# Inverse transform of a two-part kernel: a fourth table buffer, two units prepared ahead, constants and two operand stacks loaded at another time

## The chip, the cores and the metric

The kernel runs on one core of a Trainium2 chip. A core has five engines that work side by side, each in the order of its own instructions: TensorE (PE, matrix products into PSUM), VectorE (DVE), ScalarE (ACT), GpSimd (POOL) and SyncE (SP). Sixteen DMA engines move data between main memory and SBUF; in this kernel their transfers are issued by SP and by POOL. The metric is the device time in microseconds of one execution; lower is better. A profile of one execution shows what each engine did and when.

## The reference

Two independent computations share one output row. Part A is a linear-memory attention over four segments of 512 positions with 32 heads of 18 columns, part B a two-dimensional Fourier filter:

```python
# A: x @ wq, x @ wk, x @ wv, per head and segment s of four
logits = einsum("bhqd,bhkd->bhqk", qs, ks) * scale + mask
a_dot  = einsum("bhqk,bhkd->bhqd", softmax(logits), vs)
a_mem  = (phi(qs) @ M) / (phi(qs) @ z + 1e-6)      # M, z: sums over the segments before
o      = g * a_mem + (1 - g) * a_dot               # then @ wo
# B: x is 2048 x 576
X = rfft2(x) * (w_r + 1j * w_i)
y = irfft2(X, s=(2048, 576))
return concatenate([a, b], axis=-1)
```

## The kernel before

The whole program is one hand-ordered stream: generators yield between small steps, and the order in which they are drained is the order of each engine's instructions. There are four stages.

1. *Forward transform* (`FFT.forward`): 16 units, matrix products with cosine and sine tables; single-precision values are carried as a high and a low part, so that each product is three.
2. *Projections* (`ATT.projections`): for each of four segments g, nine units of queries and keys (`qk_unit`) and four blocks of values (`v_unit`), 13 units i in all. Between them the VectorE steps of the transform's middle part run as a paced background (`Pace`), the last of them the butterflies `FFT.last`, which finish the array Z in four batches b = 0..3 (`s.done` tells the last one that is finished). At unit i = 9 of segment 3 the function `hook` opens the pools of the inverse and calls `inv_setup`, which issues the transfers of two small tables and of the first per-unit tables `civ` on POOL's queue (lines 257 to 267).
3. *Inverse transform* (`FFT.inverse`, from line 284): 16 units u. Unit u takes the four-by-four entry of Z that belongs to it. `ysplit(u)` (line 275) writes its high part with two ACT copies (line 280) and its low part with two POOL subtractions (line 281); three sets of these tiles Y exist. `i2` (18 matmuls, line 296) multiplies them with the unit's table `civ` into PSUM, ACT and DVE take the result out as a high and a low part T, and two units later `i3` (14 matmuls, line 307) transforms back; ACT and DVE form the output rows, SP stores them. After unit u's second `i2` the table of unit u+3 is asked for (`load_civ`, a POOL issue); there are three table buffers. `ysplit(u+2)` is issued within unit u. The tile `p` of `i2` has two PSUM buffers under the tag `i2`, `i3`'s has two others under `i3`.
4. *Attention*: 16 stacks n of eight heads. A stack is `Qs` (110 rows) and `Ks` (110 rows), each filled by six SP transfers of 18 rows by eight heads (`stack_dmas`, issue at line 608) from the projections' result in main memory. Rows 0 to 107 hold three bfloat16 parts of the values; rows 108 and 109 hold the row maxima (`Qs`, written by `mpath`, POOL issue at line 657) and constants of -1 (`Ks`, line 558). There are three `Qs` and four `Ks` buffers. `s1(t)` computes the scores of head t for the maxima (PE line 624 and 633, with DVE at 628 and 634), `s2(t)` computes them again with the maxima subtracted and takes the exponential (lines 667 to 679).

The first ten calls of `s1` belong to stacks 0 and 1 and run during the inverse: `prologue` issues the twelve loads of stack 0 in one go before the first inverse unit; from unit 3 on, at three of the four yields of each unit, it is advanced by one step, and every `s1(t)` has three steps, 30 in all. Before the first `s1` step it calls `masks` (two ACT casts of a mask and an identity that PE's line 633 reads). At two of every three steps it takes one transfer from a list q: both halves of stack 1, the `Ks` half of stack 2, and the values of stack 1. `att_setup`, ahead of the inverse's first unit, issues the four constants of -1 on POOL's queue.

`attention` then runs 133 steps t. Eight steps belong to a stack; at each stack's first step the loads of `Qs` for stack n+2, of `Ks` for n+3 and of the values for n+2 are put into a list from which two are issued in each step. The scores `s1(t+10)` run ten steps ahead, so step 6 of the attention is the first that reads stack 2.

The lines that set this order are `if i>5 and i%4!=3: next(pr,None)` in `emit`, and `if q and i%3<2: q.pop(0)()` in `prologue`.

Of the kernel before, what the change touches and what calls it, by code (L numbers as in the profile page):

```python
# [5 lines left out]
F32=mybir.dt.float32; F32R=mybir.dt.float32r  # L6
# [96 lines left out]
class FFT:  # L103
# [152 lines left out]
    def inv_setup(s,cp):  # L256
        nc,io=s.nc,s.io
        s.cp=cp; s.civ={}
        s.itab=cp.tile([128,2,2,2,FP],F32R,name="itab",bufs=1); s.itab2=cp.tile([128,2,FP],F32R,name="itab2",bufs=1)
        nc.gpsimd.dma_start(s.itab,io["itab"].rearrange("p (h r c f) -> p h r c f",h=2,r=2,c=2))  # L260
        nc.gpsimd.dma_start(s.itab2,io["itab2"].rearrange("p (r f) -> p r f",r=2))
        for u in range(3): s.load_civ(u)
    def load_civ(s,u):
        b,a=divmod(u,4)
        cc=s.cp.tile([128,2,384],F32R,name="civ",bufs=3)
        s.nc.gpsimd.dma_start(cc,s.io["civ"][4*a+b].rearrange("p (h m) -> p h m",h=2))
        s.civ[u]=cc
    def last(s):
# [14 lines left out]
    def inverse(s,yl,pp):  # L283

        nc,io=s.nc,s.io; tab,tab2=s.itab,s.itab2; v=nc.vector
        T={}; po={}; Yt=s.Yt
        def i2(u,cs):
            Y=Yt[u]; cc=s.civ[u]
            p=pp.tile([128,len(cs),256],F32,name="i2",tag="i2")
            for k,c in enumerate(cs):  # L290
                n=0
                for (i,hl) in ((0,0),(0,1),(1,0)):
                    for q in range(2):
                        o=128 if q==0 else 0
                        m=128 if c<2 else 99
                        nc.tensor.matmul(p[:m,k],Y[i][:,q,c*128:c*128+m],cc[:,hl,o:o+256],start=n==0,stop=n==5)  # L296
                        n+=1
            return p
        def i3(u):
            h,l=T.pop(u); po[u]=[]  # L300
            for r in range(2):
                p=pp.tile([128,FP],F32,name=f"i3{r}",tag="i3"); po[u].append(p)
                w=slice(r*128,(r+1)*128)
                L=[(h[:,0,w],tab[:,0,r,0]),(h[:,1,w],tab[:,0,r,1]),(h[:,0,w],tab[:,1,r,0]),(h[:,1,w],tab[:,1,r,1]),
                   (l[:,0,w],tab[:,0,r,0]),(l[:,1,w],tab[:,0,r,1]),(h[:99,2,w],tab2[:99,r])]
                for n,(x,t) in enumerate(L):
                    nc.tensor.matmul(p,x,t,start=n==0,stop=n==6)  # L307
                yield
        def out(u):
            b,a=divmod(u,4); p=po.pop(u)  # L310
            E=yl.tile([128,FP],F32,name="E")
            nc.scalar.copy(E,p[0])
            o=yl.tile([128,2,FP],F32,name="yout",bufs=3)
            v.tensor_tensor(o[:,0],E,p[1],op=OP.add)
            v.tensor_tensor(o[:,1],E,p[1],op=OP.subtract)
            pend.append(lambda: nc.sync.dma_start(io["yb"][4*a+b],o))
        pend=[]
        def flush():
            while pend: pend.pop(0)()
        for u in range(18):  # L320
            if u>15: flush()
            if u<16:
                h=yl.tile([128,3,256],F32R,name="T0",bufs=3); l=yl.tile([128,2,256],F32R,name="T1",bufs=3)
                T[u]=(h,l)
                p=i2(u,(0,1))
                nc.scalar.copy(h[:,:2],p)
                if u+2<16: s.ysplit(u+2)
                v.tensor_tensor(l,p,h[:,:2].bitcast(F32),op=OP.subtract)
                yield
                flush()  # L330
                p=i2(u,(2,))
                Yt.pop(u); s.civ.pop(u)
                nc.scalar.copy(h[:99,2],p[:99,0])
                v.tensor_tensor(h[64:97,2],p[64:97,0],h[64:97,2].bitcast(F32),op=OP.subtract)
                if u+3<16: s.load_civ(u+3)
                yield
            if u>1:
                yield from i3(u-2)
                out(u-2)
                s.pace.take(1)  # L340
        flush()
# [35 lines left out]
class ATT:  # L377
# [176 lines left out]
    def att_setup(s,cp):  # L554
        nc,io=s.nc,s.io
        s.Qs=[cp.tile([128,8,512],BF,name=f"Qs{i}") for i in range(3)]
        s.Ks=[cp.tile([128,8,512],BF,name=f"Ks{i}") for i in range(4)]
        for i in range(4): nc.gpsimd.dma_start(s.Ks[i][108:110].rearrange("p h c -> p (h c)"),io["neg1"])
        s.mask=cp.tile([128,512],F32,name="mask"); nc.sync.dma_start(s.mask,io["mask"]); s.tri=cp.tile([128,128],BF,name="tri"); s.idb=cp.tile([128,128],BF,name="idb")
        s.bt,s.gt,s.g1=[cp.tile([128,1],F32,name=n) for n in ("bt","gt","g1")]  # L560
        nc.sync.dma_start(s.bt,io["beta"])
        d=lambda n,sh,dt: s.dp.tile(sh,dt,name=n)
        s.uD=[d(f"uD{i}",[576,512],F32) for i in range(4)]
        s.rD=[d(f"rD{i}",[32,512],F32) for i in range(4)]
        nc.sync.dma_start(s.rD[3][24:32],io["neg1"][0:1].rearrange("o (h c) -> (o h) c",c=512))
        s.dD=[None]+[d(f"dD{i}",[32,512],F32) for i in range(1,4)]
        s.rrD=[d(f"rrD{i}",[64,512],F32) for i in range(4)]
        s.rdD=[None]+[d(f"rdD{i}",[64,512],F32) for i in range(1,4)]
# [284 lines left out]
    def prologue(s):  # L853

        nc,io=s.nc,s.io
        for f in s.stack_dmas(0,0)+s.stack_dmas(0,1): f()
        yield
        s.load_v(0)
        q=s.stack_dmas(1,0)+s.stack_dmas(1,1)+s.stack_dmas(2,1)+[lambda: s.load_v(1)]
        for i in range(2): yield  # L860
        s.masks()
        i=0
        for t in range(10):
            for _ in s.s1(t):
                if q and i%3<2: q.pop(0)()
                i+=1
                yield
            if t in (3,7): m=s.mpath(t//4); next(m)
            if t in (4,8): next(m); next(m,None)
        assert not q  # L870
# [3 lines left out]
    def attention(s,tp,ps):  # L874
# [7 lines left out]
        q=[]  # L882
# [11 lines left out]
        for t in range(133):  # L894
            k,hh=divmod(t,4); n,qd=divmod(k,2); g=k//8
            if hh==0 and qd==0:
                if n+2<16: q+=s.stack_dmas(n+2,0)
                if n+3<16: q+=s.stack_dmas(n+3,1)
                if n+2<16: q.append(lambda n=n: s.load_v(n+2))
            st=t%32  # L900
            if 16<=t<21: s.pq_load(1,t-16)
            if t==34: bg.append(s.den(1,lane))
            if st==8 and g>0:
                def ln(g=g):
                    r=s.recip(s.rD[g-1],s.rrD[g-1],s.g1,False,"rr",2)
                    for i in range(8):
                        next(r); yield
                    for u in range(3): s.ux_load(g-1,u)
                    yield from r
                    bg.append(s.combine(g-1))  # L910
                    for u in range(5 if g<4 else 0): bg.append(s.mem1(g,u))
                    if g<3: bg.append(s.den(g+1,lane))
                    bg.append(s.oproj(g-1))
                lane.append(ln())
            if t==125: lane.append(s.recip(s.rD[3],s.rrD[3],s.g1,False,"rr"))
            a=s.s1(t+10) if t+10<128 else iter(())
            b=s.s2(t) if t<128 else iter(())
            if q: q.pop(0)()
            if qu: qu.pop(0)()
            steps(a,1)  # L920
            steps(b,1)
            steps(a,1)
            steps(b,1)
            if 4<=t-1<132: s.pv((t-5)//4,(t-5)%4)
            run_bg(1.2)
            steps(a,1)
            if hh==3 and m is not None: steps(m,1)
            steps(b,1)
            if hh==3 and m is not None: steps(m,1)
            if hh==1 and k+2<32: m=s.mpath(k+2); next(m)  # L930
            if t>=8 and t%4==0:
                s.pv_out((t-8)//4)
                if t%8==4:
                    u=s.u_dmas((t-12)//8)
                    if t<124: s.later(1,lambda u=u: qu.extend(u))
                    else: qu+=u
            for l in list(lane):
                try: next(l)
                except StopIteration: lane.remove(l)
            if q: q.pop(0)()  # L940
            if qu: qu.pop(0)()
            run_bg(0)
            s.due(t)
# [6 lines left out]
        i=0  # L950
# [59 lines left out]
def emit(nc,tc,io):  # L1010
    def pool(es,name,bufs=1,**kw):
        return es.enter_context(tc.tile_pool(name=name,bufs=bufs,reuse_waits="tile",**kw))
    with ExitStack() as L0:
# [9 lines left out]
        with tc.manual_schedule():  # L1023
# [5 lines left out]
            with ExitStack() as es:  # L1029
# [3 lines left out]
                def hook(g,i):  # L1033
                    if g==3 and i==9:
# [2 lines left out]
                        F.yp=pool(Ri,"yp",2); F.Yt={}; ci=pool(Ri,"ci")  # L1037
                        tc.swap_default_side()
                        F.inv_setup(ci)
                A.projections(xp,tp,pp,wv,F.pace,hook)  # L1040
                F.ysplit(0); F.ysplit(1)
            Rv.close(); L1x.close()
            with ExitStack() as L1:
                cp2=pool(L1,"cp2"); sm=pool(L1,"sm",2); sp=pool(L1,"sp",3)
# [33 lines left out]
```

## Time and profile before

| | us |
|---|---|
| three runs | 777.62, 773.33, 770.01 (median 773.33) |
| the profiled execution | 769.95 |
| its span, first to last instruction | 768.2 |
| forward transform (0 to 76.1) | 76.1 |
| projections (76.1 to 284.4) | 208.3 |
| inverse transform with the first scores (284.4 to 370.9) | 86.5 |
| attention with its last projection (370.9 to 768.2) | 397.3 |

The stage bounds are read from the timeline: the first matmul of each stage on PE, or the end of the last one of the stage before. The granted clock of TensorE was 0.989 over the span. Within the inverse PE was busy 76.53 of the 86.5 us, in the projections 206.26 of 208.3.

In the profile L296 means line 296 of the kernel; the names behind an operation are output <- inputs, by the program's names. PE is the matmuls, PEld the weight loads beside them, SPq and POOLq the issue of transfers on the queues of SP and POOL. In a timeline row the first two numbers are the start and the time taken (several instructions of one kind are merged, "x18"), and a bracket tells how long the engine stood idle before it and what ended that. A row of the chain of waits has start, time, and what the chain went through.

### The profile page before, as it was taken

Reading aid. Unit: us, or ns where it says so; the run is one execution under the profiler, and the core shown is the slowest. Engines: PE = TensorE matmul, PEld = TensorE weight load, DVE = VectorE, ACT = ScalarE, POOL = GpSimd, SP = SyncE. Lnnn points to the kernel's source line nnn. Section 1 sums busy time; section 2 is a strip of 40 time slices with the busy share of each in tenths; the row PEclk is TensorE's granted clock in tenths of the full one; section 3 lists DMA queues with packets and bytes.
Section 4 is the critical chain, followed back from the end, with each engine's and each line's share of the span. In section 5 each row is a group of like instructions: output and inputs, shape, how many; then the busy total and the mean of one; then the engine's idle time right before and its main releaser. Section 6 shows DMA issues by size and latency. Waiting matters only on the chain.

```text
span 768.2 us, 14538 instructions
## 1 busy us (share of the span) xinstructions
PE 717.4 (93%) x5007; PEld 502.4 (65%) x5007; DVE 543.7 (71%) x1266; ACT 464.1 (60%) x1012; POOL 213.2 (28%) x405
## 2 busy tenths in 40 slices
PE   4998999999999986999898999999999999998897
PEld 4987779789798785899543444444665446652386
DVE  6999878897888882886777878776557765562133
ACT  3656794775783833444576777775556665657421
POOL 2110000100101025454254334452224823238100
PEclk9999999999999998999999999999999999999999
DMA  9883535653643388665577656765356664331141
GB/s 325 272 251 124 173 131 172 209 162 125 210 166 105 138 282 190 171 207 177 141 170 180 153 138 153 193 156 145 103 138 167 150 154 118 85 106 39 34 157 62
DMA packets 81933, 121.63 MB, mean 158 GB/s; under 512 B 8280, under 2 KB 48742, under 8 KB 81724
## 3 DMA queue, kind: packets, MB, share of 16 engines
q1 hardware_dynamic: 75300, 104.63, 47.2%
q0 software_dynamic: 6560, 16.08, 7.3%
q8 instruction: 39, 0.64, 0.3%
q14 instruction: 34, 0.28, 0.1%
HBM read 81.97 MB, written 38.50 MB: 157 GB/s over the span
## 4 chain that ended last, share of the span: by engine, by line
PE 77%; DMA 6%; DVE 5%; ACT 4%; POOL 4%; issue 3%; SPq 1%; ACTq 0%; DVEq 0%; POOLq 0%
PE pj L451 13%; PE pv L694 10%; PE s L624 9%; PE pjv L451 7%; PE po L811 6%; PE i L296 4%; PE i L307 4%; PE s L667 3%; PE s L671 2%; PE f L142 2%; PE po L840 2%; PE pn L761 2%; PE s L676 2%; PE c L162 2%; PE s L633 2%
## 5 line engine op out<-in xcount | busy, mean ns | idle before, releaser
L628 DVE CUSTOM_DVE_ANT_0 junk<-s,mask 128x512 bf16<-128x512 f32 (+1 forms) x256 | 141.3, 552 | 72.2 <-PE s L624 68.8
L624 PE MATMUL s<-Ks,Qs 108*128 108x384 bf16 (+3 forms) x512 | 139.3, 305 | 4.7 <-DMA Ks<-qkD 1.9
L694 PE MATMUL pv<-P,vs 128*32 128x512 f32 (+3 forms) x1024 | 96.6, 449 | 7.3 <-POOL P L679 4.8
L679 POOL TENSOR_SCALAR_AFFINE_SELECT P<-P 128x512 f32<-128x512 f32 x128 | 77.6, 638 | 79.8 <-ACT P L668 74.4
L634 DVE TENSOR_REDUCE mx<-s 128x4 f32<-128x512 f32 x128 | 88.0, 687 | 15.4 <-PE s L633 12.8
L624 PEld LDWEIGHTS <-Qs 108*128 108x128 bf16 x512 | 50.3, 98 | 60.3 <-issue 43.8
L668 ACT ACTIVATE P<-s 128x512 f32<-128x512 f32 x128 | 76.9, 601 | 20.5 <-PE s L667 16.0
L677 ACT ACTIVATE P<-s 128x256 f32<-128x256 f32 x128 | 49.4, 386 | 56.6 <-PE s L676 56.2
L673 ACT ACTIVATE P<-s 128x512 f32<-128x512 f32 x128 | 76.5, 598 | 1.0 <-PE s L672 0.4
L451 PE MATMUL pj<-xh,wqkl 128*128 128x512 f32 x180 | 71.1, 395 | 0.0
L451 PE MATMUL pj<-xh,wqkh 128*128 128x512 f32 x180 | 71.1, 395 | 0.0
L451 PE MATMUL pj<-xl,wqkh 128*128 128x512 f32 x144 | 61.8, 429 | 0.0
L667 PE MATMUL s<-Qs,Ks 110*128 110x512 bf16 x128 | 49.3, 385 | 2.0 <-DMA Qs<-mts 1.9
L296 PE MATMUL i<-civ,Y 128*128 128x256 f32 (+1 forms) x288 | 40.9, 295 | 8.9 <-DMA civ<-civ 5.6
L206 DVE TENSOR_TENSOR Z<-t,t 128x290 f32<-128x290 f32 (+1 forms) x96 | 48.6, 555 | 0.1
L451 PE MATMUL pjv<-wvh,xh 128*128 128x288 f32 x160 | 48.1, 303 | 0.0
L451 PE MATMUL pjv<-wvl,xh 128*128 128x288 f32 x160 | 46.2, 295 | 0.0
L206 DVE TENSOR_TENSOR t<-Z 128x580 f32<-128x580 f32 x64 | 45.7, 755 | 0.0
L694 PEld LDWEIGHTS pv<-P,vs 128*32 128x32 f32 x1024 | 21.0, 108 | 36.3 <-issue 24.1
L296 PEld LDWEIGHTS i<-civ,Y 128*128 128x128 f32 (+1 forms) x288 | 37.6, 189 | 10.4 <-issue 5.8
L498 POOL MEMSET vt<- 128x32 f32 x16 | 2.3, 162 | 149.6 <-PE pm L508 128.9
L633 PE MATMUL s<-tri,idb 128*128 128x128 bf16 x256 | 43.3, 220 | 0.0
(162 smaller groups left out, 1638.3 us busy)
## 6 DMA issues: line engine op xcount, KB each, us to landing
qkD<-sp SPq DMA_DIRECT2D x36, 384.0 KB
Qs<-qkD SPq DMA_DIRECT2D x96, 144.0 KB
Ks<-qkD SPq DMA_DIRECT2D x96, 144.0 KB
xin<-xb SPq DMA_DIRECT2D x16, 384.0 KB
cfw<-cfw POOLq DMA_DIRECT2D x16, 384.0 KB, 4.5
civ<-civ POOLq DMA_DIRECT2D x16, 384.0 KB, 3.7
vs<-vD SPq DMA_DIRECT2D x16, 330.0 KB
vD<-vt SPq DMA_DIRECT2D x16, 311.0 KB
```

The source lines that it names most:

```text
L206: v.tensor_tensor(o,a,b,op=op)
L296: nc.tensor.matmul(p[:m,k],Y[i][:,q,c*128:c*128+m],cc[:,hl,o:o+256],start=n==0,stop=n==5)
L451: s.nc.tensor.matmul(out,a,b,start=i==0,stop=i==len(L)-1)
L624: nc.tensor.matmul(out,Q[:108,h,128*i:128*i+128],K[:108,h,:128*(i+1)],start=True,stop=True)
L628: nc.vector.tensor_tensor_reduce(out=junk[:,:w],in0=src,in1=s.mask[:,512-w:],scale=1.0,scalar=-3.0e38, op0=OP.add,op1=OP.max,accum_out=s.m ...
L633: nc.tensor.matmul(pa[:,o+w-128:o+w],s.idb,s.tri,start=False,stop=True,skip_group_check=True)
L634: nc.vector.tensor_reduce(out=s.mx[k][:,hh],in_=pa.rearrange("p (b c) -> p b c",c=128),axis=mybir.AxisListType.X,op=OP.max)
L667: nc.tensor.matmul(p0,kk(0),q(0),start=True,stop=True)
L668: nc.scalar.activation(P[0][:,hh],p0,AF.Exp,scale=SC)
L673: nc.scalar.activation(P[1][:,hh],p1,AF.Exp,scale=SC)
L679: sel=lambda x,pat: nc.gpsimd.affine_select(out=x,in_=x,pattern=pat+[[1,128]],compare_op=OP.is_ge,fill=0.0,base=0,channel_multiplier=-1)
L694: nc.tensor.matmul(s.pvt[32*hh:32*hh+32,128*j:],vt[:,j,19*h:19*h+32],mv[0][:,hh,mv[1]],start=jj==0,stop=jj==3,skip_group_check=True)
```

## The change

Six edits, four of them in the inverse and its setup:

- `civ` gets a fourth buffer; `inv_setup` loads four tables, and each unit asks for the table of unit u+4.
- Unit 1's `i2` tiles are taken under the PSUM tag `i3`.
- `ysplit(0)` and `ysplit(1)` are issued in the hook at units 11 and 12 of the last segment of the projections (the third and fourth block of values) and no longer after the projections.
- The four constants of -1 are issued in the prologue, after `s1(2)` to `s1(5)`, one each, and no longer in `att_setup`.
- The prologue's list also holds the `Qs` half of stack 2 and the `Ks` half of stack 3, 31 transfers instead of 19. One is taken at every step, two at steps 0 and 24.
- The attention no longer loads these two halves at its first step.

```diff
         nc.gpsimd.dma_start(s.itab2,io["itab2"].rearrange("p (r f) -> p r f",r=2))
-        for u in range(3): s.load_civ(u)
+        for u in range(4): s.load_civ(u)
     def load_civ(s,u):
         b,a=divmod(u,4)
-        cc=s.cp.tile([128,2,384],F32R,name="civ",bufs=3)
+        cc=s.cp.tile([128,2,384],F32R,name="civ",bufs=4)
...
-            p=pp.tile([128,len(cs),256],F32,name="i2",tag="i2")
+            p=pp.tile([128,len(cs),256],F32,name="i2",tag="i3" if u==1 else "i2")
...
-                if u+3<16: s.load_civ(u+3)
+                if u+4<16: s.load_civ(u+4)
...
-        for i in range(4): nc.gpsimd.dma_start(s.Ks[i][108:110].rearrange("p h c -> p (h c)"),io["neg1"])
...
-        q=s.stack_dmas(1,0)+s.stack_dmas(1,1)+s.stack_dmas(2,1)+[lambda: s.load_v(1)]
+        q=s.stack_dmas(1,0)+s.stack_dmas(1,1)+s.stack_dmas(2,0)+s.stack_dmas(2,1)+[lambda: s.load_v(1)]+s.stack_dmas(3,1)
...
             for _ in s.s1(t):
-                if q and i%3<2: q.pop(0)()
+                for _ in range(1+(i%24==0)):
+                    if q: q.pop(0)()
                 i+=1
                 yield
+            if 2<=t<6: nc.gpsimd.dma_start(s.Ks[t-2][108:110].rearrange("p h c -> p (h c)"),io["neg1"])
...
-                if n+2<16: q+=s.stack_dmas(n+2,0)
-                if n+3<16: q+=s.stack_dmas(n+3,1)
+                if 0<n<14: q+=s.stack_dmas(n+2,0)
+                if 0<n<13: q+=s.stack_dmas(n+3,1)
...
+                    if g==3 and i>10: F.ysplit(i-11)
                 A.projections(xp,tp,pp,wv,F.pace,hook)
-                F.ysplit(0); F.ysplit(1)
```

## The prediction

> **What bounds the kernel now.** I read the busy shares first, then the chain of waits, then the timeline of each engine where the chain leaves TensorE.
>
> ```profile
> PE 717.4 (93%) x5007; PEld 502.4 (65%) x5007; DVE 543.7 (71%) x1266; ACT 464.1 (60%) x1012; POOL 213.2 (28%) x405
> 284.40:370.90 86.50, 76.53 (x576) 71.48 (x576) 53.46 (x127) 35.66 (x87) 39.62 (x56) 0.96 0.65 178
> ```
>
> TensorE is busy 93% of 768.2 us. The second line is the inverse transform by the view of stretches (length, then busy time of PE, PEld, DVE, ACT, POOL, granted clock, DMA share, GB/s): PE stands 10 us of 86.5 there, and the chain in order of time says where.
>
> ```profile
> 275.12 9.31 PE pjv L451 x70
> ...
> 285.85 1.18 POOL Y L281
> ...
> 293.26 9.76 DMA civ<-civ
> 303.02 0.14 issue
> 303.16 4.11 PE i L296 x18
> 307.26 1.01 issue
> 308.28 0.32 PE s L624
> ...
> 310.95 1.42 PE i L296 x12
> 315.73 1.42 PE i L296 x12
> 362.65 2.15 PE i L296 x18
> ```
>
> The projections end on PE at 284.4. The start is paced by the low parts on POOL (L281), then by the fourth table: its load starts at 293.26, lands 9.76 us later, and unit 3 runs at 303.16. Its 18 matmuls take 4.11 us, where 18 take 2.15 at 362.65: they ran at half clock. From 308.28 on PE is full, one unit per 4.78 us (310.95 to 315.73). So only what ends before 308.28, and what comes after the inverse, can move the time.
>
> **Part by part.** *Fourth buffer.* Table 3 is issued with the first three near 270 instead of at 293.26. The wait ends, if nothing else holds PE: before it PE's last matmul ran to 297.58 (295.54+2.04, a row below), so it is 5.58 us.
>
> *Parts of units 0 and 1 earlier.* Four ACT copies and four POOL subtractions move in front of the value copies of the last two projection units.
>
> ```profile
> L280 ACT CAST Y<-Z x32: 357/490/625, 284.7 to 357.1; 128x512 fp32r<-128x512 f32 x16, 128x198 fp32r<-128x198 f32 x16
> L281 POOL TENSOR_TENSOR Y<-Z,Y x32: 570/881/1211, 285.8 to 358.8; 128x512 fp32r<-128x512 f32 x16, 128x198 fp32r<-128x198 f32 x16
> 271.33 2.91 DVE L206 TENSOR_TENSOR Z<-t,t 128x580 f32<-128x580 f32 x6
> 280.85 0.70 ACT L501 COPY vt<-pjv 128x288 f32<-128x288 f32 x2 [3.42 <-DMA vD<-vt]
> 280.89 0.16 POOL L498 MEMSET vt<- 128x32 f32 x1 [8.72 <-DMA vD<-vt]
> ```
>
> Their input is done at 274.24. They cost ACT 2 x (0.63+0.36) = 2.0 us and POOL 2 x (1.21+0.57) = 3.6 us, against holes of 3.42 and 8.72 us on the same engines, so nothing shows. If the holes were gone, up to 2 us of ACT would delay the last value copies. PE can start the inverse at 284.4 at once, and unit 1 takes two other PSUM buffers, so it need not wait until unit 0's are read. Units 0 to 3 are four times 2.15 us, unit 0's back transform is 2.04 (rows of both in the next fence): 284.4+8.6+2.04 = 295.0. The casts of the mask and identity stand behind unit 3 on ACT (they end at 308.26, 1.0 us after unit 3), so the first scores s1(0) could begin near 296.1.
>
> *What is late next.* PE takes its work in order, and s1(0) needs all of stack 0: twelve loads that SP issues when the projections are over.
>
> ```profile
> 286.88 2.44 SPq L608 DMA_DIRECT2D Qs<-qkD  x6
> 289.37 7.15 SPq L608 DMA_DIRECT2D Ks<-qkD  x6
> Ks<-qkD SPq DMA_DIRECT2D x96, 144.0 KB
> q1 hardware_dynamic: 881, 0.84, 60.8%
> ...
> q1 hardware_dynamic: 2057, 1.97, 56.4%
> q0 software_dynamic: 546, 1.23, 31.3%
> ...
> 295.54 2.04 PE L307 MATMUL i<-itab,T 128*128 128x290 f32 x14
> 307.96 0.30 ACT L573 CAST idb<-ident 128x128 bf16<-128x128 f32 x1
> 300.00:305.00 5.00, 1.84 (x8) 1.88 (x9) 0.00 (x0) 0.00 (x0) 0.00 (x0) 0.52 0.99 240
> 305.00:310.00 5.00, 3.99 (x25) 3.61 (x25) 1.81 (x3) 2.32 (x7) 2.24 (x3) 0.80 0.52 144
> ```
>
> SP issues them from 286.88 to 296.52; neither this order nor its start changes, since the value blocks of the last projections, whose end does not move, go out ahead of them. The queue lines are packets, MB and share of the 16 engines: the first for 288 to 294, when SP's queue q1 held only these loads, the other two for 288 to 305. At 0.84 MB in 6 us (0.14 MB/us), 12 x 144 KB = 1.77 MB need 12.6 us: from 288 to 300.6 at the earliest. By 305 the queue had moved 1.97 MB, 0.2 more than the twelve, but part of that belongs to later loads; just then the DMA share falls from 0.99 to 0.52. I put the landing near 305.5. The upper bound is 308.28, when s1(0) ran, plus one table: POOL's queue q0 moved 1.23 MB there, three tables of 384 KB and the constants; with PE ahead the changed kernel asks for tables 4 to 7 (384 KB more, at 240 GB/s 1.6 us). So s1(0) begins between 300.6 and 309.9; I take 306, half a table behind 305.5, nearest to the row at 305. That is 2.3 us before 308.28.
>
> *The clock.* The idle time moves from before unit 3 to before s1(0), and grows from 5.6 to 11 us.
>
> ```profile
> 300.20:307.00 6.80, 3.84 (x18) 3.87 (x18) 0.28 (x1) 0.90 (x2) 0.00 (x0) 0.50 0.87 229
> 385.50:389.00 3.50, 3.50 (x18) 1.27 (x18) 1.93 (x7) 2.12 (x5) 1.40 (x1) 0.51 0.76 185
> ```
>
> Here unit 3 paid 4.11-2.15 = 1.96 us for the half clock, ahead of 308.28; afterwards the same is paid behind 306. The half clock comes in stretches of 3.4 us (3.50 and 6.80 us are one and two): if 1.7 us of it are left when work starts it costs 0.9, if 5.1 us are left 2.6. I take 1.9, as here. The start therefore gives -2.3+1.9 = -0.4 us (bounds: -7.7+0.9 = -6.8, and +1.6+2.6 = +4.2).
>
> *Constants of -1 later.* Four issues leave POOL's queue.
>
> ```profile
> 289.42 2.03 POOL L558 DMA_DIRECT2D Ks<-neg  x4
> ```
>
> Those 2.03 us stood ahead of unit 2's parts. They move into the steady part, where POOL is busy 4.97 of 10 us (stretch from 320 below), and their rows are read only in the attention: the cost is hidden by POOL's idle half, and would be 2 us on the way to one table without it. The gain is swallowed by the wait for stack 0.
>
> *Two more stacks during the inverse.* Twelve SP issues of 144 KB leave the first steps of the attention, and what they do there is plain.
>
> ```profile
> 372.37 0.35 SPq L608 DMA_DIRECT2D Qs<-qkD  x1
> ...
> 376.19 4.80 SPq L608 DMA_DIRECT2D Ks<-qkD  x5
> 384.32 0.32 PE L624 MATMUL s<-Ks,Qs 108*128 108x384 bf16 x1 [1.88 <-DMA Ks<-qkD]
> ```
>
> Stack 2's first scores (step 6) wait 1.88 us for loads issued from 372.37 on, and the clock is then granted at 0.51 for 3.50 us, another 3.5x0.49 = 1.7. Both go: -3.6 us. Next late is the row of maxima (rival 2). In the inverse the loads rise from two to three per unit. Today's share there:
>
> ```profile
> 320.00:330.00 10.00, 10.00 (x81) 9.44 (x81) 8.91 (x23) 4.38 (x11) 4.97 (x7) 1.00 0.68 201
> civ<-civ POOLq DMA_DIRECT2D x10, 384.0 KB, 3.6
> yb<-yout SPq DMA_DIRECT2D x10, 290.0 KB
> ```
>
> 0.68 of the engines leaves room, tables land in 3.6 us (issues between 308 and 356), and after the change they are asked for about three units (14 us) ahead. PE is full, so I put the cost at zero, with rival 3 as its upper end. The row speaks of all 16 engines. The Trainium skill (DMA: Bandwidth & Descriptors, "Why a DMA increments its semaphore by 16 and not by 1") says that a transfer is split over the largest number of engines up to 16 that divides its slowest dimension; for these 18 rows that makes nine. The 60.8% with nothing else queued agrees. By the mean share the sum is -4.0, by that rule it is rival 3's.
>
> **Sum.** -0.4-3.6 = -4.0 us: span 768.2 to 764.2, the profiled execution (769.95) to 766.0. The median of the three runs, 773.33, lies 3.4 above the profiled one; 773.33-4.0 = 769.3.
>
> **Rivals.** *1, stack 0 lands early.* With the constants gone from POOL's queue and table 3 loaded before, the loads run at 0.14 MB/us throughout and land at 300.6. Then the start gives -7.7+1.9 = -5.8, in all -9.4: 763.9. For it: nothing else was moved from 288 to 294. Against: tables 4 and 5 still come in between. 15%.
>
> *2, the wait in the attention moves.* The next row of maxima is also a small transfer through a loaded queue.
>
> ```profile
> 409.50 0.61 PE L667 MATMUL s<-Qs,Ks 110*128 110x512 bf16 x1 [1.94 <-DMA Qs<-mts]
> ```
>
> Such a wait at step 8 costs 1.94+1.7 = 3.6 and eats the gain: 773.33-0.4 = 772.9. Against: with twelve loads less in the queue it should land sooner. 20%. The Trainium skill (TensorE: Matmul & The Clock Gate, "What's actually happening") gives the half rate after an idle window of some 3.4 us; here 1.88 us sufficed, so short waits are charged with the clock too.
>
> *3, slower: the engines that carry the stacks become the bound of the inverse.* One load takes 147 KB/0.14 = 1.05 us on the engines that it uses, about 0.61 of all by the 60.8%. Two loads per 4.78 us make 0.44 of these engines and 0.27 of all; the other 0.68-0.27 = 0.41 is spread evenly, so they are at 0.85 now and at 0.66+0.41 = 1.07 afterwards: 0.33 us per unit over ten units, 3.3 us. If a load costs as in the start, where twelve took from 286.9 to 305.5 beside three tables (1.55 each), three of them and an output of 290 KB at 240 GB/s (1.2) make 5.85 us per unit, +10.7 over ten. The middle is 7.0. PE feels it once a table needs more than its 14 us. Then -4.0+7.0 = +3.0: 776.3, and up to 780, more if short waits halve the clock. For it: 1.07 is over 1. Against: tables landed in 3.6 us at 0.85. 15%.
>
> **Numbers.** My forecast has 50%, its own range 765 to 774 (start from -5 to +4). What this kernel's measurement can tell from no change is about 1%, 7.7 us. Below 765.6 lie nearly all of rival 1 and a tenth of the forecast: 0.20. Above 781.1 lies rival 3 with the clock halved (0.08), and its middle with a scatter like that of the three runs, 770.01 to 777.62 (0.04): 0.12. Within: 0.68. The range takes rival 1 and the lower part of rival 3: 762 to 777.
>
> **What would show it.** Right: i2 starts within 0.2 us of the last projection; no wait for civ; PE idle from about 295, ended by Qs or Ks rows near 306, then half clock; one unit per 4.78 us afterwards; no wait at step 6 of the attention. Wrong: s1(0) before 301, units longer than 5 us or waits for civ after 310, a wait of 2 us in the attention's first ten steps.

## The result, and the profile after

| | before | changed |
|---|---|---|
| median of 17 runs each, us | 773.75 (767.8 to 781.69) | 780.23 (774.91 to 785.87) |
| ratio, with its 95% interval | 1 | 1.0086 (1.0061 to 1.0112) |
| span of the profiled execution, us | 768.2 | 773.9 |

The changed kernel is slower by 0.9%, where 0.5% faster was forecast; the time lies above the range. The profiles differ by 5.7 us. The chain of waits of the changed kernel (start, time, what the chain went through) says where they are lost:

```profile
276.69 10.24 POOL Y L281
...
287.59 0.10 POOL vt L498
...
287.73 4.21 DMA vD<-vt
...
292.33 0.41 ACT vt L501
...
293.21 0.38 SPq L558
...
294.77 0.51 SPq L607
...
305.38 10.11 DMA vs<-vD
...
315.57 0.48 PE s L623
...
325.00 1.42 PE i L296 x12
```

The chain leaves TensorE before the projections end. It runs through one POOL subtraction of 10.24 us, then the constant columns of a value block (L498, also POOL), the block's store vD, the ACT copies into the value buffer that this store sets free (L501), and SP's queue, where the loads of stack 0 (L607, line 608 before) begin at 294.77 instead of 286.88. The first scores run at 315.57 instead of 308.28, 7.3 us later.

The profile names the values' load `vs`, which SP issues right behind the twelve loads, as what released the first scores, but their code reads only `Qs` and `Ks`. The trace also keeps each load's semaphore: that of the last of the twelve is raised for the last time at 315.27, and at 307.97 before. In each of the eight kernels here in which the first scores wait, they begin 0.30 to 0.33 us after that moment, whatever the profile names as releaser. So they wait for the whole of stack 0, and they did so before the change, too. The timelines of POOL, VectorE and ACT show the subtraction in its place:

```profile
276.69 10.90 POOL L281 TENSOR_TENSOR Y<-Z,Y 128x512 fp32r<-128x512 f32 x2 [4.15 <-ACT Y L280]
287.53 0.16 POOL L498 MEMSET vt<- 128x32 f32 x1
...
276.79 2.91 DVE L206 TENSOR_TENSOR Z<-t,t 128x580 f32<-128x580 f32 x6
279.62 2.78 DVE L206 TENSOR_TENSOR t<-Z 128x580 f32<-128x580 f32 x4
282.31 2.91 DVE L206 TENSOR_TENSOR Z<-t,t 128x580 f32<-128x580 f32 x6
285.14 0.76 DVE L206 TENSOR_TENSOR t<-Z 128x580 f32<-128x580 f32 x1
...
292.04 0.70 ACT L501 COPY vt<-pjv 128x288 f32<-128x288 f32 x2 [9.65 <-DMA vD<-vt]
```

From 276.79 to 285.90 VectorE's butterflies follow each other without a gap. POOL's two subtractions for unit 0 end at 287.59, the first of them about 1 us after the last butterfly, which is what such a subtraction takes by itself (1.21 at most before). POOL had not worked for 10 us; for about 9 of them it had stood still.

The other end of the change did what it should. First value products of blocks 0 and 1 in the attention (a block is four steps; step 6 lies between the two rows), before, then after:

```profile
381.05 1.07 PE L694 MATMUL pv<-P,vs 128*32 128x512 f32 x8
...
393.30 1.07 PE L694 MATMUL pv<-P,vs 128*32 128x512 f32 x8
```

```profile
390.34 1.06 PE L693 MATMUL pv<-P,vs 128*32 128x512 f32 x8
...
398.94 1.07 PE L693 MATMUL pv<-P,vs 128*32 128x512 f32 x8
```

The changed kernel comes to block 0 9.3 us late: 7.3 us from the first scores; the rest, 2 us, fits the half clock behind them (granted 0.52 in the last fence of this section, the third number from the end). At block 1 it is 5.6 us late, so the attention's first steps gave back 9.29-5.64 = 3.65 us. The 5.6 us stay to the end. The stretch behind the first scores:

```profile
315.50:320.20 4.70, 4.63 (x21) 4.26 (x22) 1.39 (x3) 0.40 (x1) 0.00 (x0) 0.52 0.52 145
```

### The profile page after: what moved, and what is told of

The parts are those of the page before. It is cut to its first block, busy times and chain, and to the rows that moved or that the text cites. A ratio compares the mean times of both kernels' runs of the same rounds, so it can differ in the third digit from the quotient of the medians.

```text
span 773.9 us, 14535 instructions
## 1 busy us (share of the span) xinstructions
PE 715.8 (92%) x5007; PEld 503.1 (65%) x5007; DVE 543.4 (70%) x1266; ACT 463.8 (60%) x1012; POOL 222.5 (29%) x405
## 4 chain that ended last, share of the span: by engine, by line
PE 69%; DMA 10%; DVE 8%; ACT 5%; POOL 4%; issue 3%; SPq 1%; ACTq 0%; DVEq 0%; POOLq 0%
PE pj L451 13%; PE pv L693 9%; PE s L623 8%; PE po L810 6%; PE pjv L451 6%; PE i L307 4%; PE i L296 3%; PE s L666 3%; PE s L670 2%; DMA vs<-vD 2%; PE po L839 2%; PE pn L760 2%; DVE eo L125 2%; DMA Qs<-mts 2%; DMA xin<-xb 2%
## 5 line engine op out<-in xcount | busy, mean ns | idle before, releaser
L281 POOL TENSOR_TENSOR Y<-Z,Y 128x512 fp32r<-128x512 f32 (+1 forms) x32 | 37.3, 1165 | 44.9 <-ACT Y L280 43.6
L498 POOL MEMSET vt<- 128x32 f32 x16 | 2.4, 161 | 141.9 <-PE pm L508 128.6
```

## The experiments

Theory 1: the stalled subtraction holds the constant columns behind it on POOL, and with them the store, the value buffer and the loads of stack 0. Theory 2: the added table and the two moved stacks load the DMA engines and make stack 0 late. The first four kernels tell them apart. Each ratio is to the kernel before, with its 95% interval.

**Only the early parts undone** (the changed kernel otherwise).

```diff
-                    if g==3 and i>10: F.ysplit(i-11)
                 A.projections(xp,tp,pp,wv,F.pace,hook)
+                F.ysplit(0); F.ysplit(1)
```

> The changed kernel with one edit undone: the parts of units 0 and 1 are made after the projections again. Theory 1 (the low-part subtraction of unit 0 on POOL stands still beside VectorE's last butterflies, holds the constant columns of the value blocks behind it on POOL, and so their store, the free value buffer, and SP's loads of stack 0): subtractions of 0.6 to 1.3 us, first load of stack 0 near 287, first scores at 305 to 308, no wait at step 6 of the attention, span 764 to 766, ratio to before 0.993 to 0.997. Theory 2 (the added table in the projections and the two moved stacks load the DMA engines, and that makes stack 0 late): first scores still near 315, ratio near 1.008.

Measured: ratio 0.9969 (0.9934 to 1.0004), span 765.6. The timelines of POOL, SP and PE, then two stretches of PE before and behind the first scores:

```profile
285.99 3.62 POOL L281 TENSOR_TENSOR Y<-Z,Y 128x512 fp32r<-128x512 f32 x4 [1.48 <-ACT Y L280]
...
287.12 2.44 SPq L607 DMA_DIRECT2D Qs<-qkD  x6
...
307.82 0.48 PE L623 MATMUL s<-Ks,Qs 108*128 108x384 bf16 x1 [8.52 <-issue]
```

```profile
296.00:307.80 11.80, 3.30 (x27) 3.08 (x26) 3.11 (x6) 2.80 (x9) 4.97 (x7) 0.86 0.98 229
307.80:311.40 3.60, 3.58 (x16) 3.19 (x17) 1.19 (x2) 0.40 (x1) 0.00 (x0) 0.50 0.63 158
```

All four subtractions take 3.62 us together, stack 0 is asked for at 287.12, and the first scores run at 307.82. Undoing one edit takes away the whole loss. The others together gain 2.6 us between the two profiles; by the ratio, whose interval reaches 1.0004, that gain is not clear of noise. TensorE still idles through most of 296 to 307.8 and then runs at half clock. The profile names no releaser for this wait ("issue"); the last load's semaphore ends at 307.51.

**Only the early parts done** (the kernel before otherwise): the same two lines, the other way.

> The kernel before with this edit alone: the parts of units 0 and 1 in the last projections. Theory 1: the subtraction of unit 0 takes about 10 us, first load of stack 0 near 295, first scores near 315.5, the waits in the attention stay, span about 777, ratio 1.010 to 1.014. Theory 2: ratio within 0.003 of 1.

Measured: ratio 1.0173 (1.0104 to 1.0242), span 785.9.

```profile
276.90 10.88 POOL L281 TENSOR_TENSOR Y<-Z,Y 128x512 fp32r<-128x512 f32 x2 [4.69 <-ACT Y L280]
...
295.26 2.68 SPq L608 DMA_DIRECT2D Qs<-qkD  x6
...
306.74 4.18 PE L296 MATMUL i<-civ,Y 128*128 128x256 f32 x18 [3.86 <-DMA civ<-civ]
...
318.14 0.48 PE L624 MATMUL s<-Ks,Qs 108*128 108x384 bf16 x1 [7.22 <-DMA yb<-yout]
```

The subtraction stalls again. The loss is larger than expected (four runs): the first scores come 2.6 us later than in the changed kernel. Without a fourth buffer, unit 3 also waits 3.86 us for its table, and SP issues the last load of stack 0 at 306.42 instead of 302.78. What each of the two adds was not separated.

**The constant columns off POOL** (the changed kernel otherwise). This separates the stall from what stands behind it.

```diff
+        if g==3:
+            nc.scalar.activation(vv[:,:,18:19],s.ident[:,:32].rearrange("p (h c) -> p h c",c=1),AF.Copy,scale=0.0,bias=1.0)
+            nc.scalar.activation(vt[:,608:],s.ident[:,:14],AF.Copy,scale=0.0)
+        else:
+            nc.gpsimd.memset(vv[:,:,18:19],1.0)
+            nc.gpsimd.memset(vt[:,608:],0.0)
```

> The changed kernel, with the constant columns of the last segment's value blocks written by ACT and not by POOL. Theory 1: the subtraction of unit 0 still takes about 10 us, but nothing stands behind it; the value block's store goes out near 278, first load of stack 0 near 287, first scores at 305 to 308, ratio to before 0.993 to 0.997. Theory 1b (the late low parts themselves cost the time, by the first products that wait for them): first scores near 315, ratio above 1.005. Theory 2: ratio near 1.008.

Measured: ratio 0.9969 (0.9933 to 1.0006), span 767.4.

```profile
276.76 12.68 POOL L281 TENSOR_TENSOR Y<-Z,Y 128x512 fp32r<-128x512 f32 x4 [4.34 <-ACT Y L280]
...
277.52 7.98 SPq L506 DMA_DIRECT2D vD<-vt  x3
...
287.15 2.44 SPq L611 DMA_DIRECT2D Qs<-qkD  x6
...
308.61 0.48 PE L627 MATMUL s<-Ks,Qs 108*128 108x384 bf16 x1 [10.47 <-issue]
```

POOL stands still as long as before (four subtractions from 276.76 to 289.44), and the loss is gone. So neither the stall nor the late low parts cost time here, where TensorE waits 10.47 us for stack 0 in any case; what stood behind them on POOL did. Theory 1b falls with theory 2. The first scores are 0.6 us later than expected.

**No read on POOL.** The low parts of units 0 and 1 are left out; POOL fills their tiles with zeros.

```diff
-        for z,h,l in zip(X,parts(Y[0]),parts(Y[1])): nc.gpsimd.tensor_tensor(l,z,h.bitcast(F32),op=OP.subtract)
+        for z,h,l in zip(X,parts(Y[0]),parts(Y[1])): nc.gpsimd.memset(l.bitcast(F32),0.0) if u<2 else nc.gpsimd.tensor_tensor(l,z,h.bitcast(F32),op=OP.subtract)
```

> The changed kernel, with the low parts of units 0 and 1 left out: POOL writes zeros into their tiles and reads nothing. If what stands still is POOL's read of SBUF beside VectorE's instructions with two SBUF inputs: each write takes under 1 us, first scores at 305 to 308, ratio 0.993 to 0.997. If any POOL work beside a full VectorE stands still: 8 to 10 us for the first write, first scores near 315, ratio near 1.008.

Measured: ratio 0.997 (0.9936 to 1.0005), span 769.0. POOL, and VectorE beside it:

```profile
272.37 0.86 POOL L281 MEMSET Y<- 128x512 f32 x2
...
273.28 0.85 POOL L281 MEMSET Y<- 128x512 f32 x2
...
271.18 2.91 DVE L206 TENSOR_TENSOR Z<-t,t 128x580 f32<-128x580 f32 x6
...
308.86 0.48 PE L623 MATMUL s<-Ks,Qs 108*128 108x384 bf16 x1 [13.81 <-DMA vs<-vD]
```

Beside butterflies of the same kind two such writes take 0.86 us. They begin 4 us sooner than the subtractions would, since they wait for nothing from ACT, but VectorE is full there too. A full VectorE does not stop POOL's writes; what stood still in the other runs reads SBUF. The first scores are 0.9 us later than expected.

The other four ask for the price of the remaining edits, and for what the idle time ahead of the first scores is worth.

**The two moved stacks alone** (on the kernel before): the edits of the prologue's list, its loop, and the two conditions in the attention.

> The kernel before with the two moved stacks alone (lists of prologue and attention). If the moved loads fit into the inverse: one unit per 4.78 us as before, no wait at step 6 of the attention, end 3.6 us earlier, ratio 0.994 to 0.997. If the engines that carry the stacks become the bound of the inverse: units of 5 us or more, or waits for a table, ratio 1.000 to 1.008.

Measured: ratio 0.9958 (0.9925 to 0.999). From 318 to 376 TensorE waits 0.6 us in all, for nothing that a transfer brings, and the units keep their pace:

```profile
321.55 1.58 PE L296 MATMUL i<-civ,Y 128*128 128x256 f32 x12
...
326.33 1.58 PE L296 MATMUL i<-civ,Y 128*128 128x256 f32 x12
```

4.78 us per unit, as before: the loads fit, although a table now takes 6.5 us to land (issues between 308 and 356) where it took 3.6. The attention gives back the same 3.65 us: block 0 begins at 382.26, 1.21 later than before, block 1 at 390.86, 2.44 earlier. (This run's span, 771.8, is no proof of a gain: its profiled execution has a span 3.6 us longer than that of before, while its 12 runs give the ratio above.)

**The fourth table alone**, with unit 1's PSUM tag (on the kernel before).

> The kernel before with the fourth table buffer and the other PSUM tag for unit 1 alone. If the first scores wait for stack 0 whether or not unit 3 waits for its table: first scores at 306 to 309, half clock behind them, first attention score 0 to 2 us later than 371.2, ratio 0.999 to 1.003. If the wait for the table was what held the start: first scores near 300, ratio 0.988 to 0.993.

Measured: ratio 1.0026 (1.0000 to 1.0051), span 772.9.

```profile
309.19 0.48 PE L624 MATMUL s<-Ks,Qs 108*128 108x384 bf16 x1 [9.12 <-DMA Qs<-qkD]
```

The wait for the table is gone and one of 9.12 us for stack 0 has taken its place; the last load lands at 308.88, against 307.97 in the kernel before. So the visible wait for the table had hidden another that ended as late, and the edit that removes it gains nothing alone. The first scores (309.19) and the first attention score (373.90) come 0.2 and 0.7 us later than expected.

**First scores three units later**, with the parts after the projections.

```diff
-                        if i>5 and i%4!=3: next(pr,None)
+                        if i>17 and i%4!=3: next(pr,None)
```

> The changed kernel with the parts of units 0 and 1 after the projections (as in the first experiment) and the first scores three units later, so that units 4 to 6 stand ahead of the first scores in TensorE's order. If stack 0 alone holds TensorE there: TensorE is busy from 297 to 306, end 6 to 9 us earlier than in the first experiment, ratio 0.985 to 0.990. If the table of unit 4, asked for at 293 beside stack 0, is next late (it would land near 303): a wait of 4 to 6 us for civ, ratio 0.990 to 0.995.

Measured: 762.51 us, ratio 0.9867 (0.9837 to 0.9896), span 761.0. The stretch in which the first experiment stood idle:

```profile
296.00:306.00 10.00, 10.00 (x82) 10.00 (x81) 6.26 (x12) 5.53 (x14) 6.87 (x9) 1.00 0.86 242
306.00:313.30 7.30, 7.30 (x60) 7.28 (x59) 4.63 (x10) 3.36 (x9) 4.57 (x6) 1.00 0.74 207
```

TensorE is full at full clock, and there is no wait for a table. The fear of the second branch was wrong. Of the 1.3%, about 1% is this edit's (0.9867 against 0.9969 in the first experiment). Stack 0 also lands sooner, at 303.32 against 307.51: the first experiment issues loads of stack 1 beside it from 298.61 on, this kernel only from 312.70. That these slowed it was not tested.

**The same, with stack 0's loads spread and the early parts kept** (constant columns on ACT).

```diff
-        for f in s.stack_dmas(0,0)+s.stack_dmas(0,1): f()
+        for f in s.stack_dmas(0,0)+s.stack_dmas(0,1):
+            yield
+            f()
...
-                        if i>5 and i%4!=3: next(pr,None)
+                        if i<12 or i>17 and i%4!=3: next(pr,None)
```

> The changed kernel with the constant columns of the last value blocks on ACT (third experiment), the first scores three units later, and the twelve loads of stack 0 spread over units 0 to 3, one to a step, instead of in one go. If loads in one go are what makes the tables of units 4 and 5 late: tables land in under 7 us, TensorE has no wait over 2 us between 288 and 370, ratio 0.980 to 0.987. If spreading changes nothing: as the kernel with later scores alone, a wait for civ of 4 to 6 us.

Measured: 761.09 us, ratio 0.9842 (0.9802 to 0.9881), span 757.9.

```profile
283.70:288.00 4.30, 1.88 (x12) 1.48 (x11) 1.69 (x4) 0.84 (x4) 4.22 (x3) 0.93 0.50 144
288.00:296.00 8.00, 8.00 (x57) 8.00 (x57) 3.09 (x6) 5.41 (x13) 5.50 (x9) 0.83 0.74 155
296.00:306.00 10.00, 10.00 (x82) 10.00 (x81) 6.90 (x14) 4.20 (x11) 6.69 (x9) 1.00 0.99 235
```

TensorE is full from 288 on. Before that it waits for the low parts of unit 0, whose subtraction stalls here as well (276.19, 10.24 us): here the late low parts do hold TensorE. The spread did not bring the tables sooner: they land in 5.9 us at the median in both kernels (issues between 285 and 345). Both kernels beat the one before by 1.3 to 1.6%; between the two the intervals overlap, so what spreading and early parts add to the later scores stays open.

## Why the prediction was wrong

- **The step that failed** is the one on the early parts: "They cost ACT 2 x (0.63+0.36) = 2.0 us and POOL 2 x (1.21+0.57) = 3.6 us, against holes of 3.42 and 8.72 us on the same engines, so nothing shows." The holes were those engines' own idle time, and no row was asked what VectorE did in them. The first subtraction took 10.24 us instead of 1.21. The bound failed with it: it named ACT's 2 us as the price of a missing hole, and not the memset and the value store that stand behind POOL.
- **"Neither this order nor its start changes"**, said of SP's loads of stack 0, failed through the same stall: they began 7.9 us later (286.88 to 294.77). The first experiment puts them back to 287.12.
- The rows for it were in the profile of before. Two kinds of POOL addition, each twice, and what VectorE did at those times, by the two timelines:

```profile
190.87 0.43 POOL L523 TENSOR_TENSOR Mst<-mm,Mst 126x126 f32<-126x126 f32 x1 [10.62 <-DVE mm L516]
191.44 0.42 POOL L523 TENSOR_TENSOR Mst<-mm,Mst 126x126 f32<-126x126 f32 x1
192.39 0.20 POOL L524 TENSOR_TENSOR zst<-mm,zst 126x7 f32<-126x7 f32 x1
192.94 0.72 POOL L524 TENSOR_TENSOR zst<-mm,zst 126x7 f32<-126x7 f32 x1
...
191.50 0.30 DVE L516 TENSOR_TENSOR mm<-pm,bm 126x133 f32<-126x133 f32 x1 [0.52 <-POOL zst L524]
192.77 1.50 DVE L206 TENSOR_TENSOR Z<-t,t 128x580 f32<-128x580 f32 x2
```

  The addition of line 524 takes 0.20 us, and 0.72 us when it falls on a butterfly (192.77 to 194.27). A butterfly has both inputs in SBUF; beside L516, which reads one from PSUM, the addition of line 523 takes 0.42 us, as without it (0.43).
- **The fourth table: right.** Its wait ended and one for stack 0 took its place (9.12 us in the run with that edit alone).
- **First scores at 306 and the half clock's 1.9 us: mechanism right, the first size wrong.** With the early parts undone they ran at 307.82, inside the bounds of 300.6 to 309.9; the 3.60 us at 0.50 behind them cost 1.8. The forecast put the landing of stack 0 near 305.5 from rows of before, and counted 2.3 us to be gained. In that same profile its last load landed at 307.97, so there was little to gain: the first scores gained 0.46 us on 308.28, and the start came to about +1.3 instead of -0.4.
- **The moved stacks, -3.6: right.** 3.65 us by the two blocks above, in the run with this edit alone as well, and ratio 0.9958 there.
- **Constants of -1 later:** not tried alone. In the first experiment no wait on PE names them.
- **The sum:** without the early parts, -2.6 us of span where -4.0 was forecast; +1.3 for the start and -3.65 make -2.35. The loss on record comes with the early parts: ratio 1.0086 with them, 0.9969 without.
- **Rival 3, the slower one, named the wrong mechanism.** Units kept 4.78 us with three loads each; the tables landed later (6.5 us instead of 3.6) but within their 14 us. Rival 1 did not happen (stack 0 landed at 307.51 in the first experiment, not at 300.6), nor rival 2's wait at step 8: the one that its row shows belongs to step 16, and stays there at 1.30 us instead of 1.94. A rival in which a moved instruction takes longer in its new place was missing: each edit had been priced by its old durations, and only the DMA queue by what else used it.

## What to carry to other kernels

An instruction that is moved into a hole takes its duration from what runs beside it in the new place, so look up one of its kind beside the same neighbour before pricing it, and list what stands behind it on its queue down to the first transfer that another engine waits for. When a wait on the critical engine is to be removed, find what the next instruction in its order needs and when that can be there at the earliest; a wait that the profile shows can hide another that ends as late. If it does, move other work ahead of that instruction, which gave about 1% here where removing the visible wait alone gave nothing.

## What the runs showed of the hardware

A POOL subtraction that reads SBUF stood still from 276.69 until VectorE's train of butterflies ended at 285.90, although that train is seventeen separate instructions (6+4+6+1 by the rows above); it did not get in between two of them. Two POOL writes without a read took 0.86 us beside such instructions. The Trainium skill (SBUF — State Buffer, "Who interferes with whom") states that a VectorE instruction with two SBUF inputs contends with a GpSimd instruction that reads SBUF, not with one that only writes; both halves agree with these rows. The page has the one that comes second blocked until the first finishes. In the profile of before that fits: the addition that begins at 192.94 is through at 193.66, while the second of two butterflies still runs, and the next addition, which begins at 193.62, ends at 194.46, 0.19 us after that second one. In the long train it does not: the subtraction was blocked for about 9 us, and took 10.23 and 10.24 us in two other runs of the same edit. Why a long one gets no turn there is open. So is whether VectorE's second SBUF input is what matters, as the page has it: the 0.42 us beside L516 speaks for it, but no run here changed VectorE's inputs alone.

The semaphore records of the trace bear out the nine engines that the prediction took for a stack load: in the profile of before, a store of a value block raises its semaphore sixteen times (283.65 to 283.88), the last load of stack 0 once and then nine times (296.74, then 305.26 to 307.97).
